# Two pairs' value products run as one block, and a third copy of turned probabilities on VectorE

## The chip, the cores and the metric

The kernel runs on one core of a Trainium2 chip. Its time is the device time of one execution in microseconds (us). Of the kernel before there are three timed runs, 769.8, 770.33 and 771.96 us, so the median is 770.33 us. One more execution was taken with the hardware profiler.

The engines are named as the profile names them: PE (TensorE, matrix products), PEld (its weight loads, which overlap PE), DVE (VectorE), ACT (ScalarE), POOL (GpSimd) and SP (the queue that issues most DMA transfers).

## The reference, cut to what matters

The program is attention followed by a mixture of experts. Attention has 8 batches and 8 heads, 576 positions and 64 values to a head:

```python
scores = scale * np.matmul(q, k.transpose(0, 1, 3, 2))
bias = -(cum[:, :, :, None] - cum[:, :, None, :])      # cum: running sum of relu(s)
scores = np.where(causal, -1000000000.0, scores + np.minimum(bias, 0.0))
attn = np.exp(scores - np.max(scores, axis=-1, keepdims=True))
attn = attn / (np.sum(attn, axis=-1, keepdims=True) + 1e-09)
out = np.matmul(attn, v)
...
e_idx = np.argmax(x @ w_gate + modality_bias[modality_id], axis=1)
h = np.maximum(x[mask] @ w1[e], 0.0)                    # for each of 8 experts
out[mask] = gate_w[mask, None] * (h @ w2[e])
```

The change touches attention alone. The experts' part, from about 350 us on, is the same code in both kernels.

## The kernel before, in words

**Pairs.** Work goes through 32 pairs, numbered 0 to 31. A pair is one head in two batches, called a = 0 and a = 1. A pair's rows are cut into nine chunks: chunks 0 to 3 are the four blocks of 128 rows of a = 0, chunks 4 to 7 those of a = 1, and chunk 8 holds the last 64 rows of both. They run in the order 3, 7, 2, 6, 8, 1, 5, 0, 4 (`ORDER`). Because of the causal mask a chunk's width follows from its number: 512, 384, 256 and 128 columns for chunks 3, 2, 1 and 0 (and 7, 6, 5, 4), and 576 for chunk 8.

**One chunk.** `score` makes two matmuls: L381 multiplies the queries `QH` with the keys `KA`, and L403 adds the low-order parts and the bias, `QL` times `KB`. (Chunk 8 does it in two halves, L421 and L422.) The result stands in a PSUM buffer `sp`, of which there are four. DVE adds the mask and takes the row minimum (L405, L427), ACT takes the exponential (L436). Three steps later (`LAG = 3`) `trans` turns the chunk by 128x128 transposes on PE into a PSUM buffer `pt`, of which there are two (L456; L471 for chunk 8, whose last piece goes to the tile `o`), and the turned chunk is copied into `PT`. That copy is done on ACT (L460), except for chunk 8, which is on DVE (L474, L476) because `PTDVE = (8,)`. Chunks 1 and 5 are turned and copied together, and so are 0 and 4.

**Value products.** When all of a pair is turned, `whole` multiplies it with the values: 20 matmuls (L552) with 64 columns of weights each, for the two batches side by side on the PE array. Their results, `o` and a 64-wide rest `ox` in an `sp` buffer, are copied to `oT` (L559 on ACT, L562 on DVE). Four matmuls with `pw` and one with `pq` (L355) turn `oT` back, in two steps that lie some chunks apart (`XLAG = 6`), and DVE scales them into the rows `x` (L574, L576). `whole` of a pair waits one step (`TD = 1`), so its block of value products lies in the next pair, after that pair's chunk 8.

**Operands of the next pair.** While a pair runs, `prep` makes the operands of the pair after it, nearly all on POOL: two copies to `KA`, two to `QH` (L331), two differences to `QL` and two to the lower half of `KA` (L335), each time a = 0 and then a = 1. There are two sets of these tiles, used in turn, so `prep` of pair n + 1 writes what pair n - 1 has read. The order print calls them `KA_105` (even pairs) and `KA_106` (odd pairs). Chunk 3, the first of a pair, is of a = 0, and chunk 7, the second, of a = 1. DMA transfers issued by SP bring the raw queries and keys (`rawq`, `rawk`, L313), the values `V` (L318) and the pieces of `KB` and `QL`. For the first eight pairs the bias pieces come in five small transfers (L271, L290), later in two (L258, L259).

**Other work in between.** Every eight pairs, when all heads of two batches are done, their rows are routed and written to the experts' lists by nine indirect transfers on POOL (L846), which stand between the `prep` instructions of about five pairs.

**What sets the order.** The order on each engine is made when the kernel is built, by a scheduler that places an instruction when its model of the engines says that it is ready; `issue_after` adds edges that it must keep. On the chip each engine then runs its own list strictly in that order.

Of the kernel before, what the change touches and what calls it, by code (L numbers as in the profile page):

```python
# [7 lines left out]
F32 = mybir.dt.float32  # L8
# [4 lines left out]
ALU = mybir.AluOpType  # L13
# [11 lines left out]
ORDER = (3, 7, 2, 6, 8, 1, 5, 0, 4)  # L25
LAG = 3
XLAG = 6
TD = 1
SPB = 4
PTDVE = (8,)  # L30
JOINT = (0, 1)
QUIET = 4
QSTEPS = 5
# [10 lines left out]
class Attn:  # L44
# [3 lines left out]
    def __init__(self, ctx, tc, qkv, s, ident, wg):  # L48
        nc = tc.nc
# [53 lines left out]
        nb, last = t1.tile([P, 5], F32, name="nb"), 0.0  # L103
# [195 lines left out]

    def consts(self):  # L300
        nc = self.nc
        nc.gpsimd.memset(self.oT[:, 512:], 0.0)
        for t in self.PT:
            nc.vector.memset(t[64:, :, PTW - 64:], 0.0)

# [8 lines left out]
        return raw  # L314

    def load_v(self, pi):
        V = self.ld.tile([P, 2, 5, 64], F32, name="V")
        self.nc.sync.dma_start(V, self.qkv[pi, :, 4 * KW:].rearrange("p (a j d) -> p a j d", a=2, j=5))  # L318
        return V

# [209 lines left out]
        if g:  # L530
            nc.vector.tensor_scalar(x[2][:, 0, :, h], xo[:, 4 * XW:5 * XW].rearrange("p (d r) -> p d r", r=2), rs[:, 8:9], None, ALU.mult)

    def whole(self, st):

        nc = self.nc
        V, PT, x, h = st["V"], st["PT"], st["x"], st["h"]
        for _ in range(TD):
            yield
        o, ox = st["o"], self.ps1.tile([P, 512], F32, name="sp", bufs=SPB)
        oT = self.oT  # L540

        pe, self.pe = self.pe, []
        for j in range(5):
            for q0, q1, t, b in ((P * j, 512, o, 0), (512, KW, ox, 512)):
                if q0 == q1:
                    continue
                for ab in range(2):
                    r = slice(64 * ab, 64 * ab + 64)
                    with ExitStack() as after:
                        for i in pe:  # L550
                            after.enter_context(self.tc.issue_after(i))
                        m = nc.tensor.matmul(t[r, q0 - b:q1 - b], V[:, ab, j, :], PT[:, ab, PTS * j + q0 if j < 4 else PTW - 64:PTS * j + q1 if j < 4 else PTW], start=j == 0, stop=j == (4 if b else 3))  # L552
                pe = [m.ins]
        self.wall = m.ins
# [4 lines left out]
        nc.scalar.copy(oT[:, :512], o)  # L559
        for ab in range(2):  # L560
            r = slice(64 * ab, 64 * ab + 64)
            nc.vector.tensor_copy(oT[r, 512 + 64 * ab:576 + 64 * ab], ox[r, :64])  # L562
        yield
        xo = self.xo
        for g in (1, 0):
            for u in range(2):
                c = 2 * g + u
                with self.tc.issue_after(self.pe[-1]):
                    self.pw_(xo[:, 2 * XW * u:2 * XW * u + 2 * XW], oT[:, P * c:P * c + P], self.pw[:, h, :], start=True, stop=True)
            if g:  # L570
                self.pw_(xo[:, 4 * XW:5 * XW], oT[:, 512:], self.pq[:, h, :], start=True, stop=True)
            src = xo[:, :4 * XW].rearrange("p (t d) -> p t d", t=4)
            rv = rs[:, 4 * g:4 * g + 4].unsqueeze(2).broadcast_to([P, 4, XW])
            nc.vector.tensor_tensor(x[g][:, :, :, h], src.rearrange("p t (d r) -> p t d r", r=2), rv.rearrange("p t (d r) -> p t d r", r=2), ALU.mult)  # L574
            if g:
                nc.vector.tensor_scalar(x[2][:, 0, :, h], xo[:, 4 * XW:5 * XW].rearrange("p (d r) -> p d r", r=2), rs[:, 8:9], None, ALU.mult)  # L576
                for _ in range(XLAG if st["pi"] % 8 < 7 and st["pi"] < 30 else 1):
                    yield
# [5 lines left out]
    def run(self, npair, newx, done, setup):  # L584
# [5 lines left out]
        for k in range(n + LAG + 9):  # L590
# [1038 lines left out]
```

## Time and profile before

| what | value |
|---|---|
| median of the timed runs | 770.33 us (769.8 to 771.96) |
| the profiled execution | 770.52 us, span of its trace 768.8 us |
| PE busy | 759.4 us, 99% of the span |
| DVE, ACT, POOL busy | 557.6, 504.7 and 371.3 us |
| granted PE clock | 1.0 in every slice |
| attention, pairs 0 to 31 | from about 9 to 352 us |

A row of the page's fifth part or of the view by groups names a line of the kernel, the engine, the operation, the tile written and the tiles read, the shape, a count, and then busy time and the mean of one instruction in ns. A row of the timeline has a start, a duration, the instruction, how many of them follow each other, and in square brackets the idle time before and what ended it. PE's matmuls are pipelined: the duration of one is longer than the distance to the next, so the distance between two starts is what a matmul costs PE.

### The profile page before, as it was taken

The page shows a single profiled execution, that of the slowest core. Times are in us where ns is not written, and L with a number is a line of the kernel's source. Part 1 is how long each engine was busy: PE and PEld are TensorE (multiplying, and loading weights), DVE is VectorE, ACT ScalarE, POOL GpSimd, SP SyncE. Part 2 cuts the span into 40 slices and gives each one's busy share as a digit, 9 for nine tenths or more (in the row PEclk, how much of TensorE's full clock was granted, in tenths as well). Part 3 has the DMA queues.
Part 4 walks back from the last instruction along what each step waited for, and adds up shares of the span by engine and source line. Part 5 has one row for each costly group of instructions (what it writes and reads, how often), then busy time and mean ns, then how long its engine had stood idle before and what let it go on. Part 6 is the DMA issues. An engine that isn't in the chain of part 4 may idle for free.

```text
span 768.8 us, 17227 instructions
## 1 busy us (share of the span) xinstructions
PE 759.4 (99%) x5838; PEld 665.1 (87%) x5838; DVE 557.6 (73%) x1423; ACT 504.7 (66%) x1141; POOL 371.3 (48%) x386
## 2 busy tenths in 40 slices
PE   8999999999999999999999999999999999999997
PEld 7788888888888888888899999888999998888994
DVE  7686678666876678867868787977778877887720
ACT  6888888888888888886645555655556555555410
POOL 9977987898889978995621121101011111100111
PEclk9999999999999999999999999999999999999999
DMA  6567666776567766767989987987878788786672
GB/s 228 150 224 240 193 195 194 216 252 212 172 195 230 214 191 184 242 199 202 320 287 327 325 257 241 302 242 245 292 250 269 262 248 274 244 269 215 246 269 101
DMA packets 88552, 181.05 MB, mean 235 GB/s; under 512 B 14040, under 2 KB 33626, under 8 KB 88334
## 3 DMA queue, kind: packets, MB, share of 16 engines
q1 hardware_dynamic: 82654, 159.87, 66.6%
q0 software_dynamic: 5808, 20.06, 6.7%
q8 instruction: 47, 0.77, 0.4%
q14 instruction: 43, 0.35, 0.1%
HBM read 143.43 MB, written 26.67 MB: 221 GB/s over the span
## 4 chain that ended last, share of the span: by engine, by line
PE 89%; issue 4%; DMA 4%; POOL 1%; DVE 0%; POOLq 0%; ACT 0%; SPq 0%
PE y L1254 23%; PE hp L1282 23%; PE pt L456 10%; PE o L552 9%; PE sp L381 5%; PE sp L403 5%; PE ox L355 5%; PE sp L552 2%; PE sp L421 2%; PE sp L422 2%; DMA out<-ys,oi 2%; PE pt L471 2%; DMA wrbw<-in_w 1%; DMA KB<-KA 1%; PE o L471 0%
## 5 line engine op out<-in xcount | busy, mean ns | idle before, releaser
L1267 POOL DMA_INDIRECT out<-ys,oi x36 | 44.3, 1230 | 330.1 <-ACT ys L1266 241.6
L436 ACT ACTIVATE pe<-pe,mx 128x512 f32<-128x512 f32 (+3 forms) x256 | 142.7, 560 | 19.5 <-DVE mx L405 15.7
L405 DVE CUSTOM_DVE_ANT_0 pe<-sp,mk 128x512 f32<-128x512 f32 (+3 forms) x256 | 119.2, 485 | 18.4 <-PE sp L403 13.7
L1284 ACT ACTIVATE hT<-hp 128x512 fp32r<-128x512 f32 x72 | 43.1, 599 | 96.9 <-PE hp L1282 90.2
L460 ACT COPY PT<-pt 128x512 f32<-128x512 f32 (+1 forms) x192 | 96.9, 506 | 14.0 <-PE pt L456 11.2
L456 PE MATMUL pt<-ident,pe 128*128 128x128 f32 x640 | 103.6, 276 | 0.9 <-ACT PT L460 0.9
L381 PE MATMUL sp<-KA,QH 128*128 128x256 f32 (+2 forms) x256 | 98.0, 388 | 0.3 <-POOL KA L245 0.3
L1285 DVE SCALAR_TENSOR_TENSOR hT<-hp,hT 128x512 fp32r<-128x512 f32 x72 | 49.6, 689 | 61.4 <-ACT hT L1284 61.2
L335 POOL TENSOR_TENSOR QL<-rawq,QH 64x576 fp32r<-64x576 f32 x62 | 87.0, 1422 | 0.3
L335 POOL TENSOR_TENSOR KA<-rawk,KA 64x576 fp32r<-64x576 f32 x62 | 86.6, 1414 | 0.1
L1282 PE MATMUL hp<-xT,wcb 128*128 128x256 f32 x648 | 86.1, 277 | 0.0
L552 PE MATMUL o<-PT,V 128*64 128x512 f32 (+1 forms) x496 | 84.4, 440 | 0.0
L456 PEld LDWEIGHTS pt<-ident,pe 128*128 128x128 f32 x640 | 75.5, 143 | 10.2 <-ACT PT L460 1.3
L403 PE MATMUL sp<-KB,QL 76*128 76x256 f32 (+2 forms) x256 | 83.5, 328 | 0.7 <-DMA KB<-KA 0.7
L1282 PEld LDWEIGHTS hp<-xT,wcb 128*128 128x128 f32 x648 | 80.0, 188 | 0.6
L1254 PE MATMUL y<-wcb,hT 128*128 128x512 f32 x336 | 78.7, 391 | 0.0
L1254 PEld LDWEIGHTS y<-wcb,hT 128*128 128x128 f32 x336 | 62.6, 188 | 13.2
L1282 PE MATMUL hp<-xT,wca 128*128 128x256 f32 x528 | 72.2, 277 | 0.0
L552 PEld LDWEIGHTS sp<-PT,V 128*64 128x64 f32 x620 | 38.1, 137 | 33.3 <-issue 28.8
L1282 PEld LDWEIGHTS hp<-xT,wca 128*128 128x128 f32 x528 | 66.1, 188 | 0.4
L1282 PE MATMUL hp<-xT,wcc 128*128 128x256 f32 x456 | 62.5, 277 | 0.0
L1254 PE MATMUL y<-wca,hT 128*128 128x512 f32 x264 | 62.1, 391 | 0.0
(301 smaller groups left out, 1627.6 us busy)
## 6 DMA issues: line engine op xcount, KB each, us to landing
wrbw<-in_w SPq DMA_DIRECT2D x94, 512.0 KB
wraw<-in_w SPq DMA_DIRECT2D x50, 512.0 KB
rawq<-in_qkv SPq DMA_DIRECT2D x31, 576.0 KB
rawk<-in_qkv SPq DMA_DIRECT2D x31, 576.0 KB
V<-in_qkv SPq DMA_DIRECT2D x32, 320.0 KB
KB<-KA SPq DMA_DIRECT2D x62, 144.0 KB
xr<-lists SPq DMA_DIRECT2D x68, 128.0 KB
wcb<-in_w SPq DMA_DIRECT2D x10, 512.0 KB
```

Source lines behind the costliest of these rows:

```text
L335: self.last = nc.gpsimd.tensor_tensor(o, i, h, ALU.subtract).ins
L381: self.pe.append(self.nc.tensor.matmul(sp[:, :nn], QH[:, q0:q0 + P], self.KA[u][:, ab, :nn], start=True, stop=False).ins)
L403: self.pe.append(nc.tensor.matmul(sp[:, :nn], QL[:EXT, q0:q0 + P], KB[:EXT, ab, :nn], start=False, stop=True).ins)
L405: ins = nc.vector.tensor_tensor_reduce(out=t[:, :n], in0=sp[:, :n], in1=self.mk[:, 512 - n:512], scale=-0.125, scalar=3.0e38, op0=ALU.add, ...
L436: self.act = nc.scalar.activation(t[:, :n], t[:, :n], AF.Exp, bias=m, scale=-1.0, accum_out=st["sums"][:, o:o + 1]).ins
L456: self.pe.append(nc.tensor.transpose(out=pt[:, o:o + P], in_=pe[:, P * j:P * j + P], identity=self.ident).ins)
L460: return cp(w[:, :, :, v:v + P], pt[:, :n * (1 + both)].rearrange("p (a j q) -> p a j q", a=1 + both, q=P))
L552: m = nc.tensor.matmul(t[r, q0 - b:q1 - b], V[:, ab, j, :], PT[:, ab, PTS * j + q0 if j < 4 else PTW - 64:PTS * j + q1 if j < 4 else PTW], ...
L1254: self.last[0] = nc.tensor.matmul(y[u], hT[:, a, f, P * u:P * u + P], W[4 + f // 2][:, c, 512 * (f % 2):512 * (f % 2) + 512], start=f == 0 ...
L1267: self.last[2] = nc.gpsimd.indirect_dma_start(out=self.out, out_offset=bass.IndirectOffsetOnAxis(ap=oi[:, u:u + 1], axis=0), in_=ys, in_of ...
L1282: self.last[0] = nc.tensor.matmul(hp[:, u], W[k][:, a, f:f + P], xT[:, c, k], start=k == 0 and i == 0, stop=k == 3 and i == 2)
L1285: lo = self.lo = nc.vector.scalar_tensor_tensor(hT[:, 1, 2 * m:2 * m + 2], hp, 0.0, hs.bitcast(F32), ALU.max, ALU.subtract)
```

## The change

The value products of an even pair no longer run by themselves. `whole` now takes the pairs of a list: pairs 2n and 2n + 1 together (pair 30 alone), once pair 2n + 1 is all turned. Their two sets of 20 matmuls run one directly after the other, without the wait of one step, then the two copies from PSUM, then the ten matmuls with `pw` and `pq` of both, spread by the list `lag`. The even pair's `o` goes to another `sp` buffer, both rests share one `ox`, a second tile `oTb` holds the second result, and `V` has three buffers instead of two. `PTDVE` becomes `(2, 8)`, which moves the copy of chunk 2 from ACT to DVE. To make room, 8192 bytes of a partition instead of the default are set aside for the descriptors of indirect transfers.

```diff
-PTDVE = (8,)
+PTDVE = (2, 8)
...
+        self.oTb = c.tile([P, 640], F32, name="oTb")
...
-        nc.gpsimd.memset(self.oT[:, 512:], 0.0)
+        for t in (self.oT, self.oTb):
+            nc.gpsimd.memset(t[:, 512:], 0.0)
...
-        V = self.ld.tile([P, 2, 5, 64], F32, name="V")
+        V = self.ld.tile([P, 2, 5, 64], F32, name="V", bufs=3)
...
+    def whole(self, sts):
+        nc = self.nc
+        for _ in range(TD if len(sts) == 1 else 0):
+            yield
+        ox = self.ps1.tile([P, 512], F32, name="sp", bufs=SPB)
+        oTs, rss = (self.oT, self.oTb), []
+        for n, st in enumerate(sts):
+            o = st["o"] if n == len(sts) - 1 else self.ps1.tile([P, 512], F32, name="sp", bufs=SPB)
+            self.values(st, o, ox, 64 * n)
+            rss.append(self.inverse(st))
+            nc.scalar.copy(oTs[n][:, :512], o)
...
+        lag = [1] * 4 if last % 8 == 7 or last >= 28 else [XLAG] if len(sts) == 1 else [6, 3, 6, 0]
...
-                    if i0 == ORDER[-1]:
-                        prev.append((self.whole(sts[p0]), sts[p0], 0))
+                    if i0 == ORDER[-1] and (p0 % 2 or p0 == npair - 2):
+                        prev.append((self.whole([sts[p0 - 1], sts[p0]] if p0 % 2 else [sts[p0]]), sts[p0], 0))
...
-    nc = _bacc.Bacc("TRN2", target_bir_lowering=False, num_devices=1)
+    nc = _bacc.Bacc("TRN2", target_bir_lowering=False, num_devices=1, dynamic_dma_scratch_size=8192)
```

(`values` holds the old loop of the 20 matmuls, `inverse` the old reciprocal of the sums; neither is changed inside.)

The change also makes the scheduler set other orders. Lines of the changed kernel are a little further down: L381 and L403 become L383 and L405, L456 becomes L458, L471 becomes L473, L552 becomes L549, L355 becomes L357, L331 and L335 become L333 and L337, L846 becomes L870.

**PE, the block of value products.** Before, pair 17's last scores of chunk 8, the block of pair 16, and the transposes after it:

```order
L422 MATMUL sp<-KB_108,QL_104 128x288
L552 MATMUL o<-PT_109,V 64x512 x2
L552 MATMUL sp<-PT_109,V 64x64 x2
L552 MATMUL o<-PT_109,V 64x384 x2
L552 MATMUL sp<-PT_109,V 64x64 x2
L552 MATMUL o<-PT_109,V 64x256 x2
L552 MATMUL sp<-PT_109,V 64x64 x2
L552 MATMUL o<-PT_109,V 64x128 x2
L552 MATMUL sp<-PT_109,V 64x64 x4
L456 MATMUL pt<-ident,pe_3083 128x128 x4
```

Now, in pair 16, the seam between the two sets of the block of pairs 14 and 15, and its end:

```order
L549 MATMUL sp<-PT_109,V 64x128 x2
L549 MATMUL sp<-PT_109,V 64x64 x4
L549 MATMUL o<-PT_110,V 64x512 x2
L549 MATMUL sp<-PT_110,V 64x64 x2
L549 MATMUL o<-PT_110,V 64x384 x2
L549 MATMUL sp<-PT_110,V 64x64 x2
L549 MATMUL o<-PT_110,V 64x256 x2
L549 MATMUL sp<-PT_110,V 64x64 x2
L549 MATMUL o<-PT_110,V 64x128 x2
L549 MATMUL sp<-PT_110,V 64x64 x4
L458 MATMUL pt<-ident,pe_2875 128x128 x4
```

Every even pair from 2 to 30 now holds two sets, after its chunk 6; the odd pairs hold none, except pair 31, which has that of pair 30.

**PE, from an odd pair to the next even one.** The end of pair 17 and the start of pair 18, before (`KA_106` is pair 17's, `KA_105` pair 18's):

```order
L471 MATMUL pt<-ident,pep 128x128 x4
L471 MATMUL o<-ident,pep 64x128
L381 MATMUL sp<-KA_106,QH_102 128x256
L403 MATMUL sp<-KB_108,QL_104 128x256
L381 MATMUL sp<-KA_105,QH_101 128x512
L403 MATMUL sp<-KB_107,QL_103 128x512
L456 MATMUL pt<-ident,pe_3174 128x128 x2
L456 MATMUL pt<-ident,pe_3191 128x128 x2
L381 MATMUL sp<-KA_105,QH_101 128x512
```

Now:

```order
L458 MATMUL pt<-ident,pe_3093 128x128 x3
L383 MATMUL sp<-KA_106,QH_102 128x256
L405 MATMUL sp<-KB_108,QL_104 128x256
L383 MATMUL sp<-KA_105,QH_101 128x512
L473 MATMUL o<-ident,pep 64x128
L405 MATMUL sp<-KB_107,QL_103 128x512
L383 MATMUL sp<-KA_105,QH_101 128x512
L458 MATMUL pt<-ident,pe_3106 128x128 x3
L473 MATMUL pt<-ident,pep 128x128 x4
L405 MATMUL sp<-KB_107,QL_103 128x512
```

Seven transposes of pair 17 (chunks 6 and 8) have moved behind the second L383 of pair 18, which is that of chunk 7, and chunks 5 and 1 (pe_3151 and pe_3163 there) behind that. The same stands at pairs 9 to 10 and 25 to 26. From pair 1 to pair 2 the seven transposes stand behind the first L383. At most other odd pairs (5, 13, 15, 21, 23, 29) the order is nearly that of before, without the block.

**POOL, the operands of pairs 29 and 30** (`KA_106`, then `KA_105`) with the indirect transfers of the last group but one. Before:

```order
L846 DMA lists<-x,di 38912x576 x2
L331 TENSOR_SCALAR KA_106<-rawk 128x576 x2
L331 TENSOR_SCALAR QH_102<-rawq 128x576 x2
L846 DMA lists<-x,di 38912x576
L335 TENSOR_TENSOR QL_104<-rawq,QH_102 64x576 x2
L335 TENSOR_TENSOR KA_106<-rawk,KA_106 64x576
L846 DMA lists<-x,di 38912x576
L335 TENSOR_TENSOR KA_106<-rawk,KA_106 64x576
L846 DMA lists<-x,di 38912x576
L331 TENSOR_SCALAR KA_105<-rawk 128x576 x2
```

Now, with what follows for pair 30:

```order
L870 DMA lists<-x,di 38912x576 x3
L337 TENSOR_TENSOR QL_104<-rawq,QH_102 64x576 x2
L337 TENSOR_TENSOR KA_106<-rawk,KA_106 64x576
L870 DMA lists<-x,di 38912x576
L337 TENSOR_TENSOR KA_106<-rawk,KA_106 64x576
L870 DMA lists<-x,di 38912x576
L333 TENSOR_SCALAR KA_105<-rawk 128x576 x2
L333 TENSOR_SCALAR QH_101<-rawq 128x576 x2
L870 DMA lists<-x,di 38912x576
L337 TENSOR_TENSOR QL_103<-rawq,QH_101 64x576 x2
L337 TENSOR_TENSOR KA_105<-rawk,KA_105 64x576
L870 DMA lists<-x,di 38912x576
```

Two transfers have moved from ahead of pair 29's operands into them; pair 30's have the same two inside as before. Elsewhere POOL's order is that of before but for a second small memset (`oTb`).

More of the change, by code (lines that the diff above doesn't have):

```diff
@@ L531, in tail, with values @@
             nc.vector.tensor_scalar(x[2][:, 0, :, h], xo[:, 4 * XW:5 * XW].rearrange("p (d r) -> p d r", r=2), rs[:, 8:9], None, ALU.mult)
-    def whole(self, st):
+    def values(self, st, o, ox, b0):
         nc = self.nc
[L536 to L540, printed above, removed]
+        V, PT = st["V"], st["PT"]
         pe, self.pe = self.pe, []
         for j in range(5):
-            for q0, q1, t, b in ((P * j, 512, o, 0), (512, KW, ox, 512)):
+            for q0, q1, t, b in ((P * j, 512, o, 0), (512, KW, ox, 512 - b0)):
                 if q0 == q1:
@@ L553, in whole, with inverse @@
                 pe = [m.ins]
-        self.wall = m.ins
+        self.pe = pe
+    def inverse(self, st):
+        nc = self.nc
         rs = self.sm.tile([P, 9], F32, name="rs")
@@ L558, in whole @@
             nc.vector.reciprocal(rs, rs)
[L559 to L562, printed above, removed]
+        return rs
+    def whole(self, sts):
+        nc = self.nc
+        for _ in range(TD if len(sts) == 1 else 0):
[7 more added lines that the diff above has]
+            nc.scalar.copy(oTs[n][:, :512], o)
+        self.wall = self.pe[-1]
+        self.pe = []
+        for n, st in enumerate(sts):
+            for ab in range(2):
+                r = slice(64 * ab, 64 * ab + 64)
+                nc.vector.tensor_copy(oTs[n][r, 512 + 64 * ab:576 + 64 * ab], ox[r, 64 * n:64 * n + 64])
@@ L563, in whole @@
         yield
         xo = self.xo
[L565 to L578, printed above, removed]
+        last = sts[-1]["pi"]
@@ new lines, in whole @@
+        lag = [1] * 4 if last % 8 == 7 or last >= 28 else [XLAG] if len(sts) == 1 else [6, 3, 6, 0]
+        if len(sts) == 2:
+            yield
+        for st, rs, oT in zip(sts, rss, oTs):
+            x, h = st["x"], st["h"]
+            for g in (1, 0):
+                for u in range(2):
+                    c = 2 * g + u
+                    with self.tc.issue_after(self.pe[-1]):
+                        self.pw_(xo[:, 2 * XW * u:2 * XW * u + 2 * XW], oT[:, P * c:P * c + P], self.pw[:, h, :], start=True, stop=True)
+                if g:
+                    self.pw_(xo[:, 4 * XW:5 * XW], oT[:, 512:], self.pq[:, h, :], start=True, stop=True)
+                src = xo[:, :4 * XW].rearrange("p (t d) -> p t d", t=4)
+                rv = rs[:, 4 * g:4 * g + 4].unsqueeze(2).broadcast_to([P, 4, XW])
+                nc.vector.tensor_tensor(x[g][:, :, :, h], src.rearrange("p t (d r) -> p t d r", r=2), rv.rearrange("p t (d r) -> p t d r", r=2), ALU.mult)
+                if g:
+                    nc.vector.tensor_scalar(x[2][:, 0, :, h], xo[:, 4 * XW:5 * XW].rearrange("p (d r) -> p d r", r=2), rs[:, 8:9], None, ALU.mult)
+                if g or st is not sts[-1]:
+                    for _ in range(lag.pop(0)):
+                        yield
```

## The prediction

> **What bounds the kernel now.** I read the page first, for the engine that is never idle:
>
> ```profile
> PE 759.4 (99%) x5838; PEld 665.1 (87%) x5838; DVE 557.6 (73%) x1423; ACT 504.7 (66%) x1141; POOL 371.3 (48%) x386
> ```
>
> PE is busy for 99% of the span. POOL's 48% is a mean over two halves: the timelines below show it nearly full in attention and nearly empty afterwards. Next the timeline of PE around one pair (14, with its neighbours), where distances between starts are what PE pays:
>
> ```profile
> 149.78 0.40 PE L381 MATMUL sp<-KA,QH 128*128 128x512 f32 x1
> ...
> 153.84 0.30 PE L421 MATMUL sp<-KA,QH 128*128 128x288 f32 x1
> 153.97 0.30 PE L422 MATMUL sp<-KB,QL 76*128 76x288 f32 x1
> 154.20 1.08 PE L552 MATMUL o<-PT,V 128*64 128x512 f32 x4
> 155.11 0.28 PE L552 MATMUL sp<-PT,V 128*64 128x64 f32 x4
> 155.22 0.82 PE L552 MATMUL o<-PT,V 128*64 128x384 f32 x4
> 155.87 0.28 PE L552 MATMUL sp<-PT,V 128*64 128x64 f32 x4
> ...
> 156.75 0.40 PE L552 MATMUL sp<-PT,V 128*64 128x64 f32 x8
> 157.08 0.66 PE L456 MATMUL pt<-ident,pe 128*128 128x128 f32 x4
> 157.50 0.36 PE L381 MATMUL sp<-KA,QH 128*128 128x256 f32 x1
> 157.70 0.28 PE L403 MATMUL sp<-KB,QL 76*128 76x256 f32 x1
> 157.82 0.65 PE L355 MATMUL ox<-pw,oT 128*128 128x144 f32 x4
> 158.31 0.34 PE L355 MATMUL ox<-pq,oT 128*128 128x72 f32 x2
> 158.48 0.49 PE L456 MATMUL pt<-ident,pe 128*128 128x128 f32 x3
> ...
> 160.41 0.40 PE L381 MATMUL sp<-KA,QH 128*128 128x512 f32 x1
> 160.65 0.39 PE L403 MATMUL sp<-KB,QL 76*128 76x512 f32 x1
> 160.88 0.60 PE L456 MATMUL pt<-ident,pe 128*128 128x128 f32 x4
> 161.24 0.48 PE L381 MATMUL sp<-KA,QH 128*128 128x512 f32 x1
> ```
>
> No row has a bracket, so PE waits for nothing. From one first score to the next a pair costs 160.41 - 149.78 = 10.63 us. The second score (chunk 7) starts 0.83 us after the first. Last, POOL, which makes the next pair's operands, here in pair 17, whose first score is the PE row under it:
>
> ```profile
> 192.28 1.46 POOL L331 TENSOR_SCALAR KA<-rawk 128x576 fp32r<-128x576 f32 x2 [2.98 <-PE sp L381]
> 193.70 1.31 POOL L331 TENSOR_SCALAR QH<-rawq 128x576 fp32r<-128x576 f32 x2
> 194.97 2.82 POOL L335 TENSOR_TENSOR QL<-rawq,QH 64x576 fp32r<-64x576 f32 x2
> 197.74 2.81 POOL L335 TENSOR_TENSOR KA<-rawk,KA 64x576 fp32r<-64x576 f32 x2
> ```
>
> ```profile
> 192.94 0.40 PE L381 MATMUL sp<-KA,QH 128*128 128x512 f32 x1
> ```
>
> The bracket says that POOL cannot start sooner: the tiles are the ones the previous pair reads until its end. From there it needs 8.3 us. The a = 0 operands are ready about halfway through the last row, at 199.1, which is 6.2 us after the pair's start, and the a = 1 operands at 200.55, 7.6 us after it. They are wanted 10.63 and 11.46 us after it, so POOL has some 4 us in hand. This is the margin to watch.
>
> **The change part by part.**
>
> *The seams of the blocks: -4.5 us.* On the way in, L422 to L552 takes 0.23 us where L421 to L422 takes 0.13: 0.10. The first set of 512 columns takes 0.91 us, against 0.65 x 4/3 = 0.86 by the set of 384: 0.05. On the way out, the eight 64-column matmuls take 0.33 us where two times four take 0.22: 0.11. The four transposes up to L381 take 0.42 us after the block and 0.36 elsewhere: 0.06. That is about 0.30 us a block. 31 blocks become 16, and at the seam inside a joint block only the weights of one kind of matmul follow those of the same kind. 15 x 0.30 = 4.5 us. The bounds are 0.27 and 0.32 by the rounding of rows, so 4.0 to 4.8.
>
> *What the block leaves behind.* A block takes 157.08 - 154.20 = 2.88 us and with 0.15 of its seams 3.03. An odd pair without it lasts 10.63 - 3.03 = 7.60 us, an even one with two about 13.4. POOL's 8.3 us for an even pair's operands must now fit into the odd pair. In a plain odd pair they do: a = 0 is ready at 6.2 and wanted at 7.6, a = 1 ready at 7.6 and wanted at 7.6 + 0.83 = 8.4. For odd pairs' operands 13.4 us are there. So 4 us in hand become 0.8 us, and these places have less:
>
> *Pairs 10, 18 and 26: +3.0 us.* Pair 17 (as 9 and 25) gives eight transposes of 0.11 us and one group of `pw` and `pq` (158.48 - 157.82 = 0.66) to its neighbours, as the order on PE shows, and lasts only 7.60 - 0.88 - 0.66 = 6.06 us. Pair 18's first score then waits 6.25 - 6.06 = 0.2 us; its chunk 7 follows after 0.47 + 0.11 us, at 6.85, and finds its keys at 7.65: 0.8 more. 1.0 us three times.
>
> *Pairs 14, 16, 22 and 24: +1.2 us; pair 30: +1.2 us.* Here indirect transfers stand between POOL's instructions. Pair 29, which starts on PE at 321.33, shows them:
>
> ```profile
> 321.70 1.32 POOL L331 TENSOR_SCALAR KA<-rawk 128x576 fp32r<-128x576 f32 x2
> 322.99 1.30 POOL L331 TENSOR_SCALAR QH<-rawq 128x576 fp32r<-128x576 f32 x2
> 324.45 1.06 POOL L846 DMA_INDIRECT lists<-x,di  x1 [0.17 <-PE sp L403]
> 325.54 2.78 POOL L335 TENSOR_TENSOR QL<-rawq,QH 64x576 fp32r<-64x576 f32 x2
> ...
> 330.88 1.44 POOL L335 TENSOR_TENSOR KA<-rawk,KA 64x576 fp32r<-64x576 f32 x1
> ```
>
> ```profile
> 321.33 0.39 PE L381 MATMUL sp<-KA,QH 128*128 128x512 f32 x1
> ```
>
> One transfer costs about 1.25 us (QL would start at 324.26 without it). With one inside, a = 1 is ready at 8.85, less 0.1 because chunk 4's L383 comes earlier now, and wanted at 8.45: 0.3 us, four times. Pair 30's have two inside: 10.6 us from the first KA to the end. They begin 0.3 us before pair 29's start (POOL has three transfers more among pair 29's own), so a = 1 is ready at 10.3; it is wanted at 7.6 + 0.47 + 0.66 + 0.44 = 9.2, with 0.1 lost at a = 0 already: 1.2 us.
>
> *Start, pair 2: +1.6 us.* POOL's early work is one unbroken run:
>
> ```profile
> 22.48 1.31 POOL L331 TENSOR_SCALAR KA<-rawk 128x576 fp32r<-128x576 f32 x2
> ...
> 27.81 2.78 POOL L335 TENSOR_TENSOR KA<-rawk,KA 64x576 fp32r<-64x576 f32 x2
> ```
>
> ```profile
> 32.26 0.39 PE L381 MATMUL sp<-KA,QH 128*128 128x512 f32 x1
> ```
>
> Pair 2's a = 0 keys are ready at 29.2, and with the added memset (0.2) at 29.4. Before, PE reached that score at 32.26, having done the block (3.03), a `pw` and `pq` group (0.66) and seven transposes (0.76) that now come later, 4.45 us. It starts 2.8 us sooner with 4.45 us more ahead: 1.6 lost.
>
> *Pair 6: +1.5 us.* The raw keys of early pairs come late:
>
> ```profile
> 66.04 1.31 POOL L331 TENSOR_SCALAR KA<-rawk 128x576 fp32r<-128x576 f32 x2 [2.10 <-DMA rawk<-in_qkv]
> ```
>
> SP asks for them behind POOL's previous pair and five small transfers, which the change leaves at the same times. POOL needs 6.75 us for a = 0, 8.1 for a = 1: 72.8 and 74.15. Pair 5 started at 64.15 and still does (0.6 won, 1.6 lost, some `pw` work put off), so pair 6 wants them at 71.8 and 72.6 plus its own delay: 1.0 and 0.5. Pair 4's miss by the same reckoning is 0.1; left out.
>
> *The copy of chunk 2, and ACT and DVE: 0.* Rows of the view by groups, 100 to 310 us, and one of the waits:
>
> ```profile
> L460 ACT COPY PT<-pt 128x384 f32<-128x384 f32 x40 | 19.0, 478 | 1.7
> L474 DVE COPY PT<-pt 128x512 f32<-128x512 f32 x19 | 13.1, 692 | 2.3
> ```
>
> ```profile
> ACT oT L559 <- PE o L552: 24.5, 31, 0.9
> ```
>
> ACT loses 0.48 us a pair; DVE gains between 0.5 (three quarters of 692) and 0.69. ACT stands idle 0.8 us in each block and will twice as long in a joint one; in the odd pair it works almost without a break. Walking through the order, chunk 4's exponential is done 0.1 to 0.4 us before its transposes in most even pairs, so I take 0, with up to 0.2 us a joint block (3 us) as the upper end and -0.5 as the lower. Were that cover gone, ACT would set the odd pair, and what is late next is the joint block itself, which must follow those transposes. The extra `V` buffer and `sp` use are hidden by the same block. No row prices the smaller room for the descriptors of indirect transfers; those of the trace are issued without a wait beyond 0.17 us, and I take 0.
>
> One rule speaks against the copy. The Trainium skill, SBUF — State Buffer, "Who interferes with whom", says that a VectorE copy in a two-port mode takes the port pair it shares with GpSimd and that the other then fully blocks. The row for it is a chunk-8 copy that ran from 160.26 to 160.95, inside this pair:
>
> ```profile
> 159.87 1.34 POOL L331 TENSOR_SCALAR KA<-rawk 128x576 fp32r<-128x576 f32 x2
> ```
>
> ```profile
> 160.26 0.69 DVE L474 COPY PT<-pt 128x512 f32<-128x512 f32 x1
> ```
>
> 1.34 us against 1.31 at 22.48: POOL was not held. By the row the copy costs POOL nothing. By the rule, where it applies, each late place would cost up to the copy's length more, which is a rival below.
>
> *Sum.* -4.5 + 3.0 + 1.2 + 1.2 + 1.6 + 1.5 = +4.0 us. The profiled execution took 770.5 us (span 768.8), so the changed one would take 774.5; the median of the timed runs lies 0.2 lower: 774.3 us. The experts' part is the same and PE-bound, so it adds nothing.
>
> **The rivals.**
>
> *The cover holds (faster).* If POOL's operands come in time everywhere, because the places above are 1 us better than I reckon, only the seams are left: 770.3 - 4.5 = 765.8, and with pair 2's 1.6, 767.4. For it: plain odd pairs fit with 0.8 us. Against it: POOL's 8.3 us are the steadiest rows of the trace, and pair 2 and pair 10 miss by more than rounding. It decides when POOL starts 1 us earlier.
>
> *Half of it (no change).* The starts at 2 and 6 cost 3.1, and the later misses overlap with waits for ACT that give POOL time, or POOL begins a little earlier, so that 1.5 of 5.4 us are left: 770.3 - 4.5 + 4.6 = 770.4.
>
> *ACT as well, or the copy holds POOL (slower still).* ACT late by 0.2 us at each of 15 joint blocks: 774.3 + 3 = 777.3. If the copy of chunk 2 held POOL for its own length, some 0.6 us at each of the ten late places, the time would be 774.3 + 6 = 780.3; the two rows above speak against it.
>
> **How the numbers follow.** About 2.3 us (0.3%) is what a measurement can tell here. The forecast, POOL late in the short pairs, has 0.42, with its own range 772.3 to 776.5; half of it 0.26; the cover that holds 0.22; ACT as well 0.08; POOL held by the copy 0.02. Slower by over 0.3% gets 0.40 of the forecast and the last two, 0.50; the same gets 0.02 of the forecast and 0.25 of the half, 0.27; faster gets the cover and the other edge of the half, 0.23. The range from 766.5 to 777.0 leaves out about one in ten on each side.
>
> **What would show it.** Right: in the profile after, POOL's rows give no waits for PE in odd pairs, PE (or PEld) has waits for POOL `KA` L337 of about 1 us at pairs 10, 18 and 26, and at 2, 6 and 30; the step from the last 64-column matmul of the first set to the first 512 of the second is about 0.05 us; odd pairs last 6 to 8 us and even ones 13 to 14. Wrong: if PE's waits name ACT or DVE, or if pair 18 starts its chunk 7 within 7 us of pair 17's start, or if the attention part ends earlier than before by 4 us.

## The result: 13.6 us slower, and the profile after

The changed kernel takes 784.02 us (median of four runs, 781.63 to 786.91) against 771.14 us for the kernel before in the same series. The ratio of the two is put at 1.0141, 95% interval 1.0093 to 1.0189 (the two medians by themselves give 1.0167). In the series behind it the kernel before stood at 770.4 us, which makes the loss 13.6 us. The prediction had the sign (slower), with 774.3 us and a range up to 777.0; the loss is more than three times the one it reckoned. The profiled execution took 785.57 us, its span 783.9 us, 15.1 us over the span before.

The page of the kernel after has PE nearly as full as before (98% against 99%), over a longer span:

```profile
PE 764.6 (98%) x5838; PEld 663.7 (85%) x5838; DVE 564.7 (72%) x1455; ACT 489.9 (63%) x1109; POOL 370.7 (47%) x387
```

PE's 764.6 busy us are 5.2 more than before, for the same matmuls, so the view of busy time says little. Where the time went is read from the first score of a pair on PE, at four places of attention. First the kernel before (pairs 9, 25 and 31; pair 17 is the row at 192.94 in the prediction), then the kernel after (pairs 9, 17, 25, 31), timeline of PE:

```profile
107.31 0.40 PE L381 MATMUL sp<-KA,QH 128*128 128x512 f32 x1
...
278.56 0.40 PE L381 MATMUL sp<-KA,QH 128*128 128x512 f32 x1
...
342.59 0.40 PE L381 MATMUL sp<-KA,QH 128*128 128x512 f32 x1
```

```profile
112.55 0.40 PE L383 MATMUL sp<-KA,QH 128*128 128x512 f32 x1
...
200.40 0.40 PE L383 MATMUL sp<-KA,QH 128*128 128x512 f32 x1
...
288.27 0.40 PE L383 MATMUL sp<-KA,QH 128*128 128x512 f32 x1
...
355.59 0.39 PE L383 MATMUL sp<-KA,QH 128*128 128x512 f32 x1
```

Up to pair 9 the change has lost 112.55 - 107.31 = 5.2 us. Eight pairs then take 87.85 and 87.87 us, where they took 85.62 before: 2.2 us are lost in every eight pairs with their four joint blocks, evenly. The last six pairs lose 3.3 us. At pair 31 the loss is 13.0 us; pair 31 and the experts' part add 0.7 in this profile, and what lies behind PE's last matmul the other 1.4. So nearly all of it is in attention, and it is a steady loss with a bad start.

The waits of the kernel after name the engines (us in total, times, longest):

```profile
PE sp L383 <- POOL KA L337: 2.7, 4, 1.1
PE pt L458 <- ACT pe L438: 2.0, 5, 0.6
PE pt L473 <- DVE PT L462: 1.6, 1, 1.6
...
PEld pt L458 <- ACT pe L438: 6.3, 16, 0.9
...
PEld sp L383 <- POOL KA L337: 4.2, 6, 1.3
```

POOL is there, as forecast, and so are ScalarE and VectorE, which the prediction had put at nothing. But the bracketed waits of PE in these three rows sum to 6.3 us: half of the loss stands in no bracket at all. It is in steps that have become longer.

Two places show how the waits look. In pair 18 (its first score is at 206.71), chunk 7's first score waits for POOL and a transpose of chunk 4 for ScalarE, right ahead of the joint block:

```profile
208.08 0.50 PE L383 MATMUL sp<-KA,QH 128*128 128x512 f32 x1 [0.53 <-POOL KA L337]
...
211.27 0.33 PE L458 MATMUL pt<-ident,pe 128*128 128x128 f32 x1 [0.31 <-ACT pe L438]
```

Pair 18 lasts 221.49 - 206.71 = 14.78 us (pairs 10 and 26 14.78 and 14.79). In pair 3 something happens that the prediction does not contain. First PE's row, then VectorE's:

```profile
52.18 1.06 PE L473 MATMUL pt<-ident,pep 128*128 128x128 f32 x4 [1.61 <-DVE PT L462]
```

```profile
48.26 1.13 DVE L761 TENSOR_SCALAR ecap<-e 128x8 f32<-128x8 f32 x1
49.30 1.46 DVE L763 TENSOR_SCALAR ew<-e 128x8 f32<-128x8 f32 x1
...
51.59 0.54 DVE L462 COPY PT<-pt 128x384 f32<-128x384 f32 x1
```

Two routing instructions of 8 columns take 1.13 and 1.46 us on VectorE, and the copy of the third chunk, new on this engine, stands behind them. The transposes of chunk 8 need the PSUM tile that it reads, and PE waits 1.61 us. POOL's rows of the same stretch show what goes with this length:

```profile
46.54 2.81 POOL L337 TENSOR_TENSOR QL<-rawq,QH 64x576 fp32r<-64x576 f32 x2
49.30 2.79 POOL L337 TENSOR_TENSOR KA<-rawk,KA 64x576 fp32r<-64x576 f32 x2
```

VectorE's first one ends at 49.39, some 0.03 us after POOL's second subtraction for QL; the next ends at 50.76, halfway through POOL's second row and 0.03 us after the first of its two instructions. They were held while POOL worked: in an experiment below (POOL's operands), where POOL's instructions lie a little later, the same two take 0.49 and 0.16 us. That is the rule which the prediction had weighed against the copy of the third chunk (the Trainium skill, SBUF — State Buffer, "Who interferes with whom": a VectorE instruction in a two-port mode and a GpSimd one block each other). It does not hold the copy, which reads PSUM, and it does hold these two, which read and write SBUF. They were nearly as long in the kernel before (0.99 and 1.46 us, again ending 0.03 us after a POOL instruction each), where no wait of PE followed.

After that wait PE's clock falls. The view by windows (engine busy times, then PEclk, DMA share, GB/s):

```profile
50.00:52.00 2.00, 0.57 (x4) 0.31 (x3) 2.00 (x6) 0.87 (x3) 2.00 (x2) 1.00 1.12 370
52.00:54.00 2.00, 1.82 (x7) 1.63 (x8) 1.59 (x8) 1.08 (x5) 0.46 (x3) 0.57 0.98 343
54.00:55.00 1.00, 1.00 (x6) 0.89 (x5) 0.72 (x3) 0.49 (x2) 0.00 (x0) 0.50 0.59 213
55.00:56.00 1.00, 1.00 (x5) 0.85 (x5) 0.16 (x2) 0.81 (x3) 0.20 (x1) 0.65 0.19 67
56.00:58.00 2.00, 2.00 (x14) 1.37 (x14) 1.92 (x6) 1.66 (x6) 2.00 (x4) 1.00 0.01 3
```

Some 3.4 us at half clock cost about 1.7 us more. Of the four runs the two at 785.6 and 786.9 us have a mean granted clock of 0.994 to 0.995, the two at 781.6 and 782.5 us 0.999; whether the fall is missing in the latter can't be seen, as they have no trace.

### The profile page after: what moved, and what is told of

Its sections match the earlier page's. It is cut to its first block, busy times and chain, and to the rows that moved or that the text cites. A ratio compares the mean times of both kernels' runs of the same rounds, so it can differ in the third digit from the quotient of the medians.

```text
span 783.9 us, 17183 instructions
## 1 busy us (share of the span) xinstructions
PE 764.6 (98%) x5838; PEld 663.7 (85%) x5838; DVE 564.7 (72%) x1455; ACT 489.9 (63%) x1109; POOL 370.7 (47%) x387
## 4 chain that ended last, share of the span: by engine, by line
PE 76%; issue 8%; DMA 7%; POOL 4%; ACT 3%; SPq 1%; DVE 1%; POOLq 0%; ACTq 0%; DVEq 0%
PE y L1278 21%; PE hp L1306 20%; PE pt L458 7%; PE sp L549 6%; PE ox L357 4%; PE o L549 4%; PE sp L383 4%; DMA out<-ys,oi 4%; PE sp L405 4%; PE pt L473 2%; ACT pe L438 2%; PE sp L423 2%; PE sp L424 2%; POOL KA L337 1%; POOL QL L337 1%
## 5 line engine op out<-in xcount | busy, mean ns | idle before, releaser
L438 ACT ACTIVATE pe<-pe,mx 128x384 f32<-128x384 f32 (+3 forms) x256 | 142.3, 558 | 15.9 <-DVE mx L407 13.2
L407 DVE CUSTOM_DVE_ANT_0 pe<-sp,mk 128x384 f32<-128x384 f32 (+3 forms) x256 | 117.0, 484 | 12.8 <-PE sp L405 9.6
L458 PE MATMUL pt<-ident,pe 128*128 128x128 f32 x640 | 107.3, 278 | 3.3 <-ACT pe L438 2.0
L462 ACT COPY PT<-pt 128x512 f32<-128x512 f32 (+2 forms) x160 | 82.0, 514 | 34.5 <-PE pt L458 31.7
L383 PE MATMUL sp<-KA,QH 128*128 128x256 f32 (+2 forms) x256 | 96.6, 384 | 4.3 <-POOL KA L337 2.7
L458 PEld LDWEIGHTS pt<-ident,pe 128*128 128x128 f32 x640 | 76.7, 143 | 15.3 <-ACT pe L438 6.3
L337 POOL TENSOR_TENSOR QL<-rawq,QH 64x576 fp32r<-64x576 f32 x62 | 86.8, 1419 | 0.3
L337 POOL TENSOR_TENSOR KA<-rawk,KA 64x576 fp32r<-64x576 f32 x62 | 86.8, 1419 | 0.1
L405 PE MATMUL sp<-KB,QL 76*128 76x256 f32 (+2 forms) x256 | 85.9, 341 | 0.9 <-DMA KB<-KA 0.9
L549 PEld LDWEIGHTS sp<-PT,V 128*64 128x64 f32 x860 | 45.8, 137 | 36.7 <-issue 25.4
L549 PE MATMUL sp<-PT,V 128*64 128x64 f32 (+1 forms) x860 | 64.4, 282 | 0.0
L1278 PE MATMUL y<-wcc,hT 128*128 128x512 f32 x264 | 62.2, 392 | 0.0
```

The source lines that it names most:

```text
L337: self.last = nc.gpsimd.tensor_tensor(o, i, h, ALU.subtract).ins
L383: self.pe.append(self.nc.tensor.matmul(sp[:, :nn], QH[:, q0:q0 + P], self.KA[u][:, ab, :nn], start=True, stop=False).ins)
L405: self.pe.append(nc.tensor.matmul(sp[:, :nn], QL[:EXT, q0:q0 + P], KB[:EXT, ab, :nn], start=False, stop=True).ins)
L407: ins = nc.vector.tensor_tensor_reduce(out=t[:, :n], in0=sp[:, :n], in1=self.mk[:, 512 - n:512], scale=-0.125, scalar=3.0e38, op0=ALU.add, ...
L438: self.act = nc.scalar.activation(t[:, :n], t[:, :n], AF.Exp, bias=m, scale=-1.0, accum_out=st["sums"][:, o:o + 1]).ins
L458: self.pe.append(nc.tensor.transpose(out=pt[:, o:o + P], in_=pe[:, P * j:P * j + P], identity=self.ident).ins)
```

## The experiments

Two theories followed from this profile. A: POOL's operands come late in short odd pairs, and, apart from it, VectorE's copy stood behind routing work in pair 3. B: ScalarE's exponentials are what the joint block waits for. Times are medians of four runs; the kernel before took 770.4 to 770.5 us beside them.

### The two parts of the change, each alone

The joint blocks with the copy back on ScalarE:

```diff
 (kernel after)
-PTDVE = (2, 8)
+PTDVE = (8,)
```

> The joint blocks stay; the copy of the third chunk goes back to ScalarE. Theory A (two separate causes: operands of POOL late in short odd pairs, and, apart from it, VectorE's copy of the third chunk queued behind the two routing instructions at pair 3): PE's wait of 1.61 us at 52.18 us and the granted clock of 0.5 to 0.65 behind it go, the waits for POOL KA L337 at pairs 2, 10, 18 and 26 stay at 1.1 and 0.5 us: about 779 us, with all runs within 1 us. Theory B (ScalarE is what the joint block waits for, because its exponentials come late): ScalarE has 0.48 us more in every pair, and the wait of pt L458 for ACT pe L438 grows by some 0.3 us at each of 15 joint blocks: 783 us or more.

Measured: 784.03 us, ratio 1.0171 (1.0152 to 1.0189). Pair 3's wait for VectorE is gone, as A has it, and the time is not better. Nor does B hold as put: PEld's waits of the transposes for ScalarE's exponentials fall to 2.0 us and those for its copies come to 4.4, where the kernel after has 6.3 and 1.1. POOL's waits took the place of pair 3's. PE's longest waits in this run:

```profile
75.45 0.50 PE L383 MATMUL sp<-KA,QH 128*128 128x512 f32 x1 [1.86 <-POOL KA L337]
...
341.41 0.50 PE L383 MATMUL sp<-KA,QH 128*128 128x512 f32 x1 [1.42 <-POOL KA L337]
```

These are pairs 6 and 30: the two places that the prediction had named (1.5 and 1.2 us) and that the kernel after does not show. There the delay of pair 3 gave POOL the time, and probably ScalarE's of 0.65 us in pair 29 did. A wait that is taken away at one place comes back at the next narrow one.

The copy on VectorE alone, with blocks of one pair:

```diff
 (kernel before)
-PTDVE = (8,)
+PTDVE = (2, 8)
```

> The kernel before with the copy of the third chunk on VectorE, and blocks of one pair as before. Theory A: the routing instructions hold VectorE for 2.5 us here too, at pair 3, so PE waits there, up to 1.6 us, and the clock may fall behind it (1.8 us more); elsewhere nothing: 770.3 to 774. Theory B: ScalarE has 0.48 us less a pair, nothing waits for it: 770.3, no wait in pair 3.

Measured: 775.16 us, ratio 1.0054 (1.0036 to 1.0072). Neither theory: PE does not wait in pair 3, where the two routing instructions take 0.24 and 0.16 us this time, and yet 4.8 us are lost. They are spread: an ordinary pair lasts 10.78 us instead of 10.63. The end of pair 13 in this run (pair 14 starts at 162.65), timeline of PE:

```profile
161.68 0.28 PE L403 MATMUL sp<-KB,QL 76*128 76x256 f32 x1
161.80 0.27 PE L471 MATMUL o<-ident,pep 128*64 128x128 f32 x1
161.83 0.36 PE L381 MATMUL sp<-KA,QH 128*128 128x256 f32 x1
162.04 0.66 PE L471 MATMUL pt<-ident,pep 128*128 128x128 f32 x4
162.45 0.36 PE L403 MATMUL sp<-KB,QL 76*128 76x256 f32 x1
162.65 0.40 PE L381 MATMUL sp<-KA,QH 128*128 128x512 f32 x1
```

The transposes of chunk 8 stand between the two products of one score (L381 and L403); in the kernel before they stand ahead of both. Step by step against that kernel, 0.06 us of a pair's loss is here and 0.10 in two steps at the transposes early in the pair. At those, weight loads wait some 0.2 us for ScalarE's exponential (PEld pt L456 for ACT pe L436, 14 times and 2.8 us in all between 109 and 281 us); the kernel before has no such wait there. ScalarE has less to do and comes later at this place. Whether the order or the copy itself costs this was the next question. It is the kernel above with the order held:

```diff
 (kernel with the copy alone)
-STRICT = [k for k in range(9, 72) if k % 9 < 4]
+STRICT = [k for k in range(9, 288) if k % 9 == 8 or k < 72 and k % 9 < 4]
 ...
-                    self.pe.append(nc.tensor.transpose(out=pt[:kp, ...
+                    with self.tc.issue_after(self.pe[-1]) if nj == 1 else ExitStack():
+                        self.pe.append(nc.tensor.transpose(out=pt[:kp, ...
```

> The kernel before with the copy of the third chunk on VectorE, as in the run with the copy alone (775.2 us), and with PE's order held at the end of a pair: the transposes of chunk 8 stay ahead of the last score, as in the kernel before, where with the copy on VectorE they stood between that score's two products. Theory O (PE's order costs the time: 0.14 us a pair in some 28 pairs): 771 to 772 us, and no new wait. Theory Q (the copy itself is late in VectorE's queue, behind the products with rs, and chunk 8's transposes need the tile it reads): PE waits 0.1 to 0.2 us for DVE PT L460 at the end of every pair, and the time stays at 774 to 776 us.

Measured: 778.88 us, ratio 1.0102 (1.0081 to 1.0122). Worse by 3.7 us than with the order let go, so theory O falls, and above the 774 to 776 us of theory Q. PE and VectorE at the end of pair 13:

```profile
163.41 0.28 PE L403 MATMUL sp<-KB,QL 76*128 76x256 f32 x1
163.76 0.65 PE L472 MATMUL pt<-ident,pep 128*128 128x128 f32 x4
164.25 0.27 PE L472 MATMUL o<-ident,pep 128*64 128x128 f32 x1
```

```profile
162.58 0.46 DVE L575 TENSOR_TENSOR x<-ox,rs 128x288 f32<-128x288 f32 x1 [0.23 <-PE ox L355]
162.96 0.28 DVE L577 TENSOR_SCALAR xq<-ox,rs 128x72 f32<-128x72 f32 x1
163.16 0.55 DVE L460 COPY PT<-pt 128x384 f32<-128x384 f32 x1
```

The copy waits on VectorE until the two products with `rs` are through and ends at 163.71; the transposes start at 163.76, 0.35 us after L403 where 0.12 is usual. No bracket says so, since PE's modelled end covers the gap; PEld's waits do (pt L472 for DVE PT L460, 18 times, 5.0 us). Theory Q has the mechanism right and its size wrong: the copy is late because of what stands ahead of it in VectorE's queue, and the order with the parted score was already the cheaper way around it. The first of the four transposes takes 0.16 us to the next in both runs, where 0.11 is usual; since here they do not part a score, the 0.06 us is not shown to be the price of the parting.

### VectorE's routing instructions

```diff
 (kernel after)
-        nc.vector.tensor_scalar(self.ecap, self.e, float(CAP), None, ALU.mult)
+        nc.gpsimd.tensor_scalar(self.ecap, self.e, float(CAP), None, ALU.mult)
 ...
-        nc.vector.tensor_scalar(self.ew, self.e, -1.0, 8.0, ALU.mult, ALU.add)
+        nc.gpsimd.tensor_scalar(self.ew, self.e, -1.0, 8.0, ALU.mult, ALU.add)
```

> The changed kernel, with the two routing instructions that took 1.13 and 1.46 us on VectorE (ecap and ew) on POOL. Theory A: PE does not wait at 52 us and the granted clock stays at 1.00 there, in every run: 784.0 - 1.6 - 1.8 = 780.6 at most, 779.9 from the fastest run's 781.6 less 1.6, and the runs within 1 us of each other instead of 5. If VectorE was late there for another reason, the wait stays and the time is 782 to 786.

Measured: 783.23 us (780.24 to 784.56), ratio 1.0156 (1.0134 to 1.0178). Pair 3's wait and its clock are gone, so its cause is shown; the gain is not there. Pair 6 takes it:

```profile
74.60 0.50 PE L383 MATMUL sp<-KA,QH 128*128 128x512 f32 x1 [1.54 <-POOL KA L337]
```

and behind this wait the clock falls as well (0.50 from 76 to 79 us). At pair 9 this kernel is 1.1 us later than the kernel after.

### POOL's operands

POOL gets less to do: its subtraction for KA is cut to 128 of 576 columns from pair 3 on, which leaves the other columns at the high half.

```diff
 (kernel after; and the same cut in the joint kernel with the copy on ScalarE)
-            low(KA[lo, a], rk[lo, a], KAf[lo, a])
+            n = KW if pi < 3 else 128
+            low(KA[lo, a, :n], rk[lo, a, :n], KAf[lo, a, :n])
```

> The changed kernel, with POOL's subtraction for the low half of KA on 128 of 576 columns from pair 3 on (the other columns keep the high half: this part of the computation is left out), so that POOL needs some 2.1 us less a pair. Theory A: the waits at pairs 10, 18 and 26 go, with what follows in them (1.47 us over a quiet pair each), and the small excess of pairs 12, 14, 16, 20, 22, 24 and 30 (0.2 to 0.3 us each): about -6 us, 778 us; pair 3's wait stays. Theory B: only POOL's own 0.53 us at three pairs go (-1.6), ScalarE's waits stay: 782 us.

Measured: 778.09 us, ratio 1.0099 (1.0082 to 1.0116): 5.9 us better than the kernel after, the number of theory A. Pairs 18 and 26 last 13.93 and 13.92 us instead of 14.78 and 14.79, pair 10 14.07, and pairs 14, 16, 22 and 24 0.17 to 0.18 us less each. That makes 3.2 us at the places that theory A had named, with pair 30's 0.1, where it had some 6. Pairs 3 and 4 together are 3.2 us shorter, and pair 5 is 1.6 longer, as pair 6 then waits 1.43 us for its keys. Theory A had left pair 3's wait in place; it is gone because POOL comes later there:

```profile
47.32 2.81 POOL L337 TENSOR_TENSOR QL<-rawq,QH 64x576 fp32r<-64x576 f32 x2
```

```profile
48.28 0.49 DVE L762 TENSOR_SCALAR ecap<-e 128x8 f32<-128x8 f32 x1
48.68 0.16 DVE L764 TENSOR_SCALAR ew<-e 128x8 f32<-128x8 f32 x1
```

These subtractions for QL are not cut and are as long as before, but they start at 47.32 instead of 46.54. VectorE's first instruction is held until 0.03 us after the first of them ends, and its second starts just ahead of the next. That the total agrees with theory A's is therefore luck in part. And 0.35 us of ScalarE's wait stays in pair 18, and 7.7 us of the loss are left.

> Joint blocks with the copy of the third chunk on ScalarE, and POOL's subtraction for KA on 128 columns only (the rest is left out), beside the same with the copy on VectorE, 778.1 us. If ScalarE's 0.48 us a pair is what the joint block then waits for: 781 us or more, with waits of pt L458 for ACT pe. If VectorE's queue is what costs (3.9 us from the copy alone, by the run with the copy alone): 774 us.

Measured: 776.60 us, ratio 1.0073 (1.0055 to 1.0092): between the two bounds, 1.5 us better than with the copy on VectorE. So the cut for POOL is worth 784.0 - 776.6 = 7.4 us in the joint kernel with the copy on ScalarE, and with POOL relieved the copy on VectorE costs 1.5 us, not 0. Without POOL's and the copy's part, 6.2 us of loss are left.

### The short odd pairs

The output products of the pairs ahead of a group's end are spaced regularly, so that pairs 9, 17 and 25 keep theirs:

```diff
 (kernel after; and with the cut for POOL)
-        lag = [1] * 4 if last % 8 == 7 or last >= 28 else ...
+        lag = [1] * 4 if last >= 28 else ...
```

> The changed kernel, with the regular spacing of the output products (6, 3, 6 steps) at the end of the first three groups of eight pairs too, so that pairs 9, 17 and 25 keep two groups of pw and pq and last some 7.7 instead of 6.3 us. Theory A (POOL late in the short odd pairs): the 0.53 us waits at pairs 10, 18 and 26 and most of the 1.47 us there go: 784.0 - 4 = 780 us. Rival: the loss there is VectorE's, which has the routing of the group and three exponentials' inputs to make in the odd pair, and moves along with it: 783 to 785 us.

Measured: 800.61 us, ratio 1.0400 (1.0367 to 1.0433). At the place in question theory A holds: pair 9 lasts 7.80 us and pair 10 12.84, together 20.64 against 6.30 + 14.78 = 21.08, and no wait for POOL is left at 10, 18 and 26. The output products now meet the routing, which uses the same PSUM tile, and both come late at the end:

```profile
230.29 0.76 PE L357 MATMUL ox<-pw,oTb 128*128 128x144 f32 x4 [1.34 <-DVE ox L854]
...
382.83 1.33 PE L357 MATMUL ox<-pw,oT 128*128 128x144 f32 x4 [8.70 <-DVE xq L599]
```

Behind these waits and one of 2.60 us for pair 30's keys the granted clock falls too: it is 0.52 from 338 to 345 us, 0.51 from 349 to 352 and 0.52 from 379 to 386.

> The regular spacing of the output products and POOL's subtraction for KA on 128 columns together (that part of the computation is left out). If what POOL's relief left at pairs 10, 18 and 26 (0.7 us each) and 11, 19 and 27 (0.5 us each) comes from the short odd pair ahead of them: 778.1 - 3 = 775 us. If it comes from VectorE's routing work, wherever it falls: 777 to 779 us.

Measured: 803.20 us, ratio 1.0427 (1.0366 to 1.0488), with waits of 1.4 and 9.2 us at the same places. As a test of what is left in pairs 11, 19 and 27 it is inconclusive, since those waits cover it.

### Both feeders light

Last, POOL and ScalarE are both cut, in the joint kernel (copy on ScalarE) and in the kernel before: beside the cut for KA the exponential is taken on the second half of each of the chunks 0 to 7 only, the first halves are left as they are.

```diff
 (joint kernel with the copy on ScalarE, and kernel before, both with the cut for POOL)
+                e0 = n // 2 if i < 8 else 0
-                self.act = nc.scalar.activation(t[:, :n], t[:, :n], AF.Exp, ...
+                self.act = nc.scalar.activation(t[:, e0:n], t[:, e0:n], AF.Exp, ...
```

> Joint blocks with the copy of the third chunk on ScalarE, POOL's subtraction for KA on 128 columns, and ScalarE's exponential on the second half of each of the chunks 0 to 7 only (the other halves of the subtraction and of the exponentials are left out), so that POOL and ScalarE are both well ahead. If only late feeders stand between the joint block and its saving at the seams (0.22 us a block by the steps on PE, 15 blocks, 3.3 us), less what the start keeps (1.2 us at pair 2, where POOL's work is whole): 768 to 769 us, and 0.9 us less than the kernel before in every eight pairs. If PE's own order is what costs (more changes between scores and transposes): 773 us or more.

> The kernel before with the same two cuts (subtraction for KA on 128 columns, exponentials on half of each chunk; the rest is left out). PE was busy 99% of the span and waited for neither, so lighter feeders bring nothing: 769.5 to 770.5 us. It is the measure for the joint kernel with the same cuts.

Measured: 1040.24 and 1039.99 us. The whole times are of no use: PE has 6234 matmuls in both instead of 5838, and the experts' part takes far longer; that these values make the routing fill the experts unevenly is likely, and not shown. The attention part is the measurement. First scores of pairs 9 and 25, joint and then single blocks:

```profile
108.38 0.40 PE L384 MATMUL sp<-KA,QH 128*128 128x512 f32 x1
...
279.65 0.40 PE L384 MATMUL sp<-KA,QH 128*128 128x512 f32 x1
```

```profile
109.08 0.40 PE L382 MATMUL sp<-KA,QH 128*128 128x512 f32 x1
...
280.03 0.39 PE L382 MATMUL sp<-KA,QH 128*128 128x512 f32 x1
```

16 pairs take 171.27 us with joint blocks and 170.95 with single ones. With both cuts the joint block still brings nothing, where the seams alone should bring 1.8 us. The expectation is not met. Yet the test is not clean: the cut leaves ScalarE's copies whole, and between 108.4 and 280 us of the joint run weight loads of chunk 8's transposes still wait for those copies (PEld pt L475 for ACT PT L464, 6 times, 1.3 us) and those of `pw` for VectorE (0.4 us), which the single blocks don't have. The scheduler also set PE's order a little differently: some 50 of the 1524 matmuls of these pairs stand elsewhere than in the joint kernel with the copy on ScalarE alone. So late feeders still hold it in part, and their share has not been parted from that of PE's own order. The cuts also bring the single blocks 0.3 us in these pairs (171.25 before), though PE's rows of that stretch have no bracket in either: small waits may hide there too, where the prediction read that PE waits for nothing.

The same 16 pairs (9 to 25) order what each cause is worth there, from the first scores of those pairs in each run:

| kernel | 16 pairs, us | over the kernel before |
|---|---|---|
| before | 171.25 | |
| single blocks, POOL and ScalarE cut | 170.95 | -0.3 |
| joint, POOL and ScalarE cut | 171.27 | 0.0 |
| joint, POOL cut, copy on ScalarE | 172.21 | 1.0 |
| joint, POOL cut, copy on VectorE | 173.34 | 2.1 |
| joint, copy on ScalarE | 174.48 | 3.2 |
| after (joint, copy on VectorE) | 175.72 | 4.5 |
| single blocks, copy on VectorE | 172.81 | 1.6 |

## Why the prediction was wrong, by its own steps

**The seams, -4.5 us.** The saving is real and smaller, and it does not stay. In the kernel after, the joint block in pair 12 and the steps at its ends:

```profile
145.50 0.34 PE L405 MATMUL sp<-KB,QL 76*128 76x384 f32 x1
145.78 2.96 PE L549 MATMUL sp<-PT,V 128*64 128x512 f32 x36
148.56 1.03 PE L549 MATMUL o<-PT,V 128*64 128x512 f32 x4
149.42 0.28 PE L549 MATMUL sp<-PT,V 128*64 128x64 f32 x4
...
151.07 0.40 PE L549 MATMUL sp<-PT,V 128*64 128x64 f32 x8
151.40 0.66 PE L458 MATMUL pt<-ident,pe 128*128 128x128 f32 x4
```

From L405 to the transposes it takes 151.40 - 145.50 = 5.90 us, where two single ones took 2 x (157.08 - 153.97) = 6.22. Of the 0.32 the ordinary step from a score to a transpose that now stands where a block's entry was takes 0.12 back: 0.20. By all steps of eight pairs (9 to 16), entries take 1.07 us instead of 1.79 and exits 0.61 instead of 1.22; less some 0.45 us for the ordinary steps in their places this is 0.22 us a block and 3.3 us in 15, not 4.5. The step of 0.05 us inside the block was right. What the prediction missed is that the rest of PE's order changes with the block. Counted over PE's rows from pair 1 to 31, the first product of a score is followed by something other than its second 44 times, 4 times before; with both feeders light the steps outside the blocks still give back 1.0 us in every eight pairs, all of the saving and a little more. Whether this is the order itself, or ScalarE's copies and VectorE, which no run relieved, is open; the waits of PEld in that run say that it is in part the latter. The prediction took only the seams out of PE's stream and let the remainder stand as it was.

**The copy of chunk 2, 0 (with 3 us as the upper end).** This is the step that failed most plainly. It compared busy times (0.48 us off ScalarE, 0.5 to 0.69 more on VectorE) and never asked where in VectorE's queue the copy would stand, and which tile it would hold. The copy costs 4.8 us alone, 1.5 us in the joint kernel with POOL relieved, and nothing over the whole kernel as it stands (784.02 against 784.03), because there ScalarE and POOL are late with or without it. In the 16 pairs it is 1.2 us. In pair 3 it brings 1.61 us and the clock's 1.7.

**POOL late in odd pairs, +3.0, +1.2, +1.2, +1.6, +1.5: 8.5 us.** The mechanism is shown, and the size was too large: less work for POOL brings 5.9 and 7.4 us (of the 5.9, 1.6 from pairs 3 to 5, by the shift in time told above), and the named places come up. Taken one by one: pair 2 waits 1.14 us (1.6 reckoned); pairs 10, 18 and 26 get 0.7 to 0.9 us back with POOL's cut (1.0); pairs 14, 16, 22 and 24 0.17 (0.3); pair 30 0.1 (1.2) and pair 6 nothing (1.5) in the kernel after, and 1.42 and 1.54 to 1.86 us in the variants without the delays ahead of them. The split was off by a little: pair 18's first score did not wait, its chunk 7 came 208.08 - 200.40 = 7.68 us after pair 17's start. That is over the 7 us that would have refuted it.

**ACT and DVE, 0.** Wrong, and named in the prediction as what would show it so. With POOL relieved, the cut on ScalarE brings 0.9 us in 16 pairs; the same two cuts bring the kernel before 0.3. The cover, exponentials 0.1 to 0.4 us ahead of their transposes, is gone at 16 transposes of the kernel after (PEld's 6.3 us): odd pairs of 6.3 to 7.8 us leave ScalarE and VectorE a shorter time for the same work. The rival on ScalarE, 0.2 us a joint block, had the mechanism with chance 0.08 and priced it alone. The rival with the copy that holds POOL did not happen: the port held VectorE, at two other instructions.

**The sum.** -4.5 + 8.5 = +4.0 became +13.0 at pair 31. From the runs: seams -3.3; PE's other steps, with or without VectorE, some +3.9 (1.04 us in eight pairs, 30 pairs); ScalarE's exponentials +1.2 (0.32 in eight, 0.47 less the 0.15 of the kernel before); the copy +2.7 (0.38 at pair 1, 0.62 in eight); POOL +4.9 at its own places, pair 8 among them; pairs 3 and 4 +3.8. That makes 13.2, an estimate that scales eight steady pairs to all, against 13.0 measured. Against the prediction's terms: PE's own steps came out at +0.6 instead of -4.5, 5.1 us worse; ScalarE, VectorE and pairs 3 and 4, which it had put at nothing, brought 7.7; and POOL brought 3.6 less than the 8.5 reckoned.

**The range** ended at 777.0, as the two cases above it (777.3 and 780.3) had 0.10 between them. Each rival moved one cause; none had several small ones at once, each on a different engine, which is what a pair of 7.6 us in place of 10.6 does to all of them. No run here beats the kernel before: each part alone loses, and joint blocks with both feeders light stay 0.3 us in 16 pairs behind single ones with the same cuts.

## What to carry to other kernels

When a change gathers an engine's work into longer blocks, every other engine's mean load stays and its window shrinks: check each of them, not only the slowest, against the shortest window. An instruction moved to an engine with room is priced by its place in that engine's queue and by the tile that it keeps from others, not by its busy time; and where waits stand in series, taking one away shows the next, so a sum of places is not the sum of their gains.

## What the runs showed of the hardware

- A wait of PE of 1.54 to 1.86 us was followed by a granted clock of 0.50 for some 3.4 us in five kernels: from 52 (kernel after), 76 (copy back on ScalarE), 76 (routing on POOL), 337 (regular spacing with POOL's cut) and 23 us (kernel before with both cuts); after single waits of 1.43 us (POOL's cut, pair 6) and less it stayed at 1.00. The Trainium skill, TensorE: Matmul & The Clock Gate, "Part 1: The HAM clock gate", puts the fall after an idle window of about 3.4 us; the return after 3.4 us agrees, and for the fall the measurement decides: less than half of that was enough here.
- Two VectorE instructions on 8 columns, from SBUF to SBUF, took 1.13 and 1.46 us, each ending 0.03 us after the POOL instruction of 1.42 us that ran beside it. With POOL's cut they took 0.49 us, ending in the same way, and 0.16 us, begun just ahead of a POOL instruction. A copy of 384 columns out of PSUM took 0.54 us beside the same POOL work.
- A wait of PE can stand in no bracket of PE's timeline, as the ends of its matmuls are modelled. With the copy on VectorE and the order held, chunk 8's transposes start 0.35 us after the matmul ahead of them, where 0.12 is usual; PEld's waits name the copy (18 times, 5.0 us), and in PE's rows only the distances between starts show it.
